# First feed-forward of a nine-tile attention and two-FFN kernel: upper output weights times both parts of the squared values in one 512-column product

## The chip, the cores and the metric

The kernel runs on one core of one Trainium2 chip. The metric is the device time of one execution in microseconds. Three runs of the kernel before gave 950.99, 953.79 and 956.82 us. One further execution was recorded by the hardware profiler, and all rows below come from that one.

## The reference

```python
x = out_up + out_local          # pooled attention plus a 7-wide local attention, heads joined: 2304 tokens x 512
h = x @ w_in                    # 512 x 2048
r = np.maximum(h, 0.0)
g = r * r
x2 = g @ w_out                  # 2048 x 512: the product that is changed
out = ((x2 @ w_a) * (x2 @ w_b)) @ w_out2    # 512 x 1536, twice, and 1536 x 512
```

All is float32. The kernel computes each matrix product to more than the precision of one pass: every operand is held as an upper part and a remainder ("hi" and "lo"), and a product is the sum of three passes, upper weights times upper values, upper weights times lower values, lower weights times upper values (`PASSES`, L188).

## The kernel before

**Tiles and stages.** The 2304 tokens are cut into nine tiles of 256 (`NT1`, `T1`). For each tile the first feed-forward runs 16 iterations f (`F1`), one for each 128 of the 2048 hidden channels; the loop counter is `it = 16 i + f` for tile i. Tiles 0 and 1 are emitted in an order written out by hand (`ORDER`), tiles 2 to 8 by the loop at L904. After the last tile the PSUM pools are closed and the second feed-forward begins with the chains of L925 (512 columns each), which take their eight banks from a new pool, `ps2`; it waits for each old bank by itself.

**One iteration.** `Hidden` (L587) runs 12 matmuls of 256 columns on TensorE (PE) into a bank h. ScalarE (ACT) then applies Relu, Square and a copy to the upper part of g (L601 to L604), and VectorE (DVE) subtracts to get the lower part (`low`, L607). That subtraction is the last reader of the bank h. Two iterations later (`LAG = 2`) `project` (L611) runs another 12 matmuls of 256 columns: for each of four blocks of 128 output channels (et) the three passes. The sums of a tile, x2, stay in two banks of 512 columns, each shared by two blocks, for 16 iterations, and `store_x2` then copies them out, one bank with ACT and one with DVE.

**Order in the loop at L904.** In iteration it: first the events of kind 0; then `Hidden(it)` and its ACT work; then the events of kind 1, which are small products on PE; then `low(it)`; then `project(it - 2)`. Each engine works its instructions off in this order.

**The events.** `Local(i)` is the local attention of tile i, done during tile i-1 (`steps`, L353). DVE multiplies and sums the scores (L373, L382) in steps 0 to 7 and multiplies by the values (L413) in steps 10 to 13, one of four head groups in each; GpSimd (POOL) adds the seven products of each (L421 to L424). The value products have two buffers `pv`, so the third multiplication waits until POOL is done with the first, and the fourth for the second. Step 14 transposes the first half on PE into a bank `xps` (L431); step 15, `assemble`, adds the pooled part on DVE (L445), copies the upper part with ACT (L450) and subtracts on DVE (L451), which frees that bank. Steps 17 and 18 do the same for the second half. Step k of tile i stands at iteration 16 (i-1) - 4 + k for k < 14 and i > 3, otherwise at 16 (i-1) - 3 + k. So the four value multiplications fall at f = 6 to 9 of tiles 3 to 7. `Pooled` is the pooled attention of one batch entry: its batches 2 and 3 run in tiles 2 and 3 and in tiles 4 and 5. Each group of two heads takes a bank for two products of scores (L254, freed by the exponentials L275), for two transposes (L302, freed by the copies L130 to aT) and for the product with the values (L316).

**The banks.** PSUM has eight banks. `ps_h` has three for h, `ps_x` two for x2, and `ps_a` three for all the small products and transposes. A tile of a pool takes a bank that is free, and its first matmul waits until the last reader of the tile before has finished. The three lines are

```python
    ps_h = pp.enter_context(tc.tile_pool(name="ps_h", bufs=3, space=PSUM))
    ps_x = pp.enter_context(tc.tile_pool(name="ps_x", bufs=1, space=PSUM))   # two tags
    ps_a = pp.enter_context(tc.tile_pool(name="ps_a", bufs=3, space=PSUM))
```

Of the kernel before, what the change touches and what calls it, by code (L numbers as in the profile page):

```python
# [17 lines left out]
P = 128  # L18
B, H, S, D = 4, 8, 576, 64
# [7 lines left out]
T1 = 256  # L27
NT1 = NT // T1
G1 = T1 // FACTOR
F1 = 2048 // P  # L30
F2 = 1536 // P
NCT = DM // P
PE_TILES = 2
# [34 lines left out]
L.18 P.16.xy H.20 L.19 J.20 P.17 P.18 P.19 H.21 L.20 J.21 H.22 J.22 P.20 H.23 J.23 H.24 L.22 L.21 J.24 L.24 L.23  # L68
# [14 lines left out]
def pooled_local_attention_two_ffn(  # L83
# [19 lines left out]
    nc = tc.nc  # L103
# [3 lines left out]
    wz = ctx.enter_context(tc.tile_pool(name="wz", bufs=4))  # L107
# [16 lines left out]
    x2_d = dr.tile([P, NCT, NT], F32, name="x2_d")  # L124
# [3 lines left out]
    def copy(engine, out, in_, scale=1.0):  # L128
# [4 lines left out]
        else:  # L133
            engine.tensor_scalar_mul(out=out, in0=in_, scalar1=scale)

    def bank(kind):
        pool, tag = {"a": (ps_a, "aux"), "h": (ps_h, "h"), "x": (ps_x, "x20"), "y": (ps_x, "x21")}[kind]
        return pool.tile([P, 512], F32, tag=tag, name="bank")


# [47 lines left out]
    PASSES = ((0, 0), (0, 1), (1, 0))  # L188
# [392 lines left out]
    wo = [Weight(w_out[f]) for f in range(F1)]  # L581
# [4 lines left out]

    class Hidden:  # L587
        def __init__(self, i, f):
            self.h = h = bank("h")[:, :T1]
# [20 lines left out]

    def project(x2, f, g):  # L611
        for et in range(NCT):
            for n, (a, b) in enumerate(PASSES):
                nc.tensor.matmul(  # L614
                    out=x2[et // 2][:, et % 2 * T1:(et % 2 + 1) * T1],
                    lhsT=wo[f].w[:, a, et * P:(et + 1) * P], rhs=g[:, b],
                    start=(f == 0 and n == 0 and et % 2 == 0), stop=(f == F1 - 1 and n == 2),
                    skip_group_check=True,
                )


    def store_x2(i, x2):
        for e2 in range(2):
            if i == NT1 - 1:
                x = wz.tile([P, 2, 2, T1], F32R, tag="w", name="xr2")
                xr2.append(x)
                split(
                    x[:, 0].rearrange("p e t -> p (e t)"), x[:, 1].rearrange("p e t -> p (e t)"), x2[e2]
                )
                continue  # L630
            if i == NT1 - 2:
                o = wr.tile([P, 512], F32, tag="w", name="x2sb")
            else:
                o = st.tile([P, 1024], F32, tag="stage", name="x2sb")[:, :512]
            if e2:
                nc.vector.tensor_copy(out=o, in_=x2[e2])
            else:
                nc.scalar.activation(out=o, in_=x2[e2], func=AF.Copy)
            nc.sync.dma_start(
                out=x2_d[:, 2 * e2:2 * e2 + 2, i * T1:(i + 1) * T1],  # L640
                in_=o.rearrange("p (e t) -> p e t", e=2),
            )


    events = {}
# [3 lines left out]
    def at_iteration(it, fn, kind=0):  # L649
        events.setdefault(it, ([], [], []))[kind].append(fn)  # L650
# [3 lines left out]
    for b in range(1, B):  # L654
        p = pooled[b]
        start = (2 * b - 2) * F1
# [6 lines left out]
                at_iteration(start + k, fn, takes)  # L663
    for i in range(PE_TILES, NT1):
        for k, fn in sorted(Local(i).steps.items()):
            at_iteration((i - 1) * F1 - (4 if i > PE_TILES + 1 and k < 14 else 3) + k, fn, k in (14, 17))
    for n in range(2):
        at_iteration((PE_TILES - 1) * F1 - 5, lambda n=n: load_qk(4 * PE_TILES + n))
        at_iteration((PE_TILES - 1) * F1 - 2, lambda n=n: load_v(4 * PE_TILES + n))
# [42 lines left out]
    hid, x2 = {}, {}  # L712
# [7 lines left out]
        hid[it].high()  # L720
        run_events(sum(hasattr(h, "g") for h in hid.values()) - 1, 1)

    def project_tile(it, kinds="xy"):
        i, f = divmod(it, F1)
        if f == 0:
            x2[i] = [bank(kind) for kind in kinds]
        project(x2[i], f, hid[it].g)
        if f == F1 - 1:
            store_x2(i, x2.pop(i))
# [13 lines left out]
    def warm(_, n, kind):  # L743
# [206 lines left out]
    for job in JOBS.split():  # L950
        at, name, j = int(job[3:]), job[0], int(job[1])
# [378 lines left out]
```

## Time and profile before

| what | value |
|---|---|
| median of three runs (lowest, highest) | 953.79 us (950.99, 956.82) |
| the profiled execution: its own time | 949.86 us |
| the profiled execution: its span, first to last instruction | 948.1 us |
| mean granted TensorE clock | 0.986 |
| PE busy | 895.6 us, 94% of the span |
| DVE, ACT, POOL busy | 692.6, 503.4, 391.8 us |

The page says how long each engine was busy and, for its costliest groups of instructions, how many there are, the mean time of one, and what ended the idle time in front of them. The times of matmuls overlap: the start of one to the start of the next is what a matmul costs in a dense run, and the timeline's merged lines give it.

### The profile page before, as it was taken

What the parts mean: (1) busy time and instruction counts of PE and PEld (TensorE: products, weight loads), DVE (VectorE), ACT (ScalarE), POOL (GpSimd) and SP (SyncE); (2) the same over time, 40 slices, a digit from 0 to 9 for tenths busy, and PEclk for the clock granted to TensorE, in tenths of its full rate; (3) what the DMA queues carried; (4) which work ended last, traced back from release to release, by engine and by line L of the source; (5) the groups of instructions that cost most, each with busy time, mean ns of one, the idle gap of its engine ahead of it and who ended that gap; (6) DMA issues with size and microseconds to landing.
All of it is one profiled execution on the core that took longest, in us unless ns stands there. A gap on an engine that the chain in (4) does not pass through costs nothing.

```text
span 948.1 us, 16541 instructions
## 1 busy us (share of the span) xinstructions
PE 895.6 (94%) x6130; PEld 813.0 (86%) x6130; DVE 692.6 (73%) x975; ACT 503.4 (53%) x1280; POOL 391.8 (41%) x352
## 2 busy tenths in 40 slices
PE   3567899999999999999999999999999999999998
PEld 3457799999999899999999987888888888788888
DVE  3687997678778686878747699898977774665451
ACT  3676985345644465443448656655555552464531
POOL 1645525526092804535353536665565450001010
PEclk9958999999999999999999999999999999999999
DMA  9669732742139221232214314875756659999522
GB/s 291 192 193 261 258 110 62 170 123 69 62 96 211 56 82 49 69 89 69 76 58 148 112 60 148 296 258 177 254 199 213 223 189 347 383 408 353 239 99 79
DMA packets 69888, 161.88 MB, mean 171 GB/s; under 512 B 8472, under 2 KB 16920, under 8 KB 69808
## 3 DMA queue, kind: packets, MB, share of 16 engines
q1 hardware_dynamic: 64336, 142.33, 43.9%
q0 software_dynamic: 2880, 10.03, 5.9%
q10 hardware_dynamic: 2592, 8.47, 2.6%
q8 instruction: 48, 0.79, 0.3%
q14 instruction: 32, 0.26, 0.1%
HBM read 115.71 MB, written 45.09 MB: 170 GB/s over the span
## 4 chain that ended last, share of the span: by engine, by line
PE 77%; DVE 7%; POOL 6%; DMA 6%; issue 2%; ACT 2%; ACTq 0%; SPq 0%; DVEq 0%; POOLq 0%
PE bank L925 39%; PE bank L614 17%; PE bank L593 16%; DMA more<-in_qk_p 2%; POOL pv L422 2%; DVE pv L413 2%; DMA qkd<-in_qk_p 2%; POOL pv L421 2%; PE bank L254 1%; DMA raw<-in_w_in 1%; PE bank L316 1%; DMA raw<-in_w_out 1%; DVE xb L785 1%; POOL x L424 1%; POOL pv L423 1%
## 5 line engine op out<-in xcount | busy, mean ns | idle before, releaser
L593 PE MATMUL bank<-xx,w 128*128 128x256 f32 x1728 | 234.7, 286 | 7.5 <-DVE g L607 2.7
L614 PE MATMUL bank<-g,w 128*128 128x256 f32 x1728 | 233.5, 286 | 3.2 <-DVE g L607 3.2
L925 PE MATMUL bank<-xb,wb 128*128 128x512 f32 x1008 | 231.3, 390 | 1.5 <-ACT r L1021 0.8
L593 PEld LDWEIGHTS bank<-xx,w 128*128 128x128 f32 x1728 | 219.6, 194 | 10.8 <-DVE g L607 3.6
L925 PEld LDWEIGHTS bank<-xb,wb 128*128 128x128 f32 x1008 | 188.4, 188 | 42.2 <-DVE r L975 1.9
L614 PEld LDWEIGHTS bank<-g,w 128*128 128x128 f32 x1728 | 216.2, 191 | 8.7 <-issue 3.9
L925 PE MATMUL bank<-op,wo 128*128 128x512 f32 (+1 forms) x648 | 132.1, 366 | 1.6 <-DVE op L785 1.6
L925 PEld LDWEIGHTS bank<-op,wo 128*128 128x128 f32 x648 | 111.9, 189 | 21.8 <-DVE op L785 2.2
L601 ACT ACTIVATE bank<-bank 128x256 f32<-128x256 f32 x144 | 53.1, 369 | 135.8 <-PE bank L593 133.4
L421 POOL TENSOR_TENSOR pv<-pv 128x768 f32<-128x768 f32 x28 | 55.0, 1963 | 168.9 <-DVE pv L413 168.9
L785 POOL TENSOR_TENSOR wb<-raw,wb 128x256 fp32r<-128x256 f32 x96 | 88.3, 941 | 55.8 <-ACT wb L865 49.6
L607 DVE TENSOR_TENSOR g<-bank,g 128x256 fp32r<-128x256 f32 x144 | 59.3, 418 | 66.7 <-ACT g L604 66.1
L413 DVE TENSOR_TENSOR pv<-vt,sc 128x1792 f32<-128x1792 f32 x28 | 81.0, 2899 | 19.1 <-POOL x L424 19.1
L1021 ACT ACTIVATE r<-bank 128x512 f32<-128x512 f32 x72 | 42.8, 595 | 73.4 <-PE bank L925 71.9
L785 DVE TENSOR_TENSOR op<-ys,op 128x512 fp32r<-128x512 f32 x84 | 54.0, 708 | 31.3 <-ACT op L788 31.3
L788 ACT ACTIVATE op<-ys 128x512 fp32r<-128x512 f32 x84 | 47.1, 624 | 26.1 <-PE bank L925 14.6
L373 DVE TENSOR_TENSOR p<-qt,kt 128x1792 f32<-128x1792 f32 x28 | 59.4, 2121 | 0.0
L130 ACT ACTIVATE raw<-raw 128x512 uint32<-128x512 uint32 (+1 forms) x87 | 53.2, 669 | 9.7 <-DMA raw<-in_w_in 7.4
L785 POOL TENSOR_TENSOR wos<-raw,wos 128x256 fp32r<-128x256 f32 x48 | 46.2, 982 | 28.8 <-ACT wos L865 25.7
L604 ACT ACTIVATE g<-bank 128x256 fp32r<-128x256 f32 x144 | 55.3, 384 | 4.6
L422 POOL TENSOR_TENSOR pv<-pv 128x256 f32<-128x256 f32 x28 | 55.5, 1983 | 2.2
L382 DVE TENSOR_REDUCE sc<-p 128x28 f32<-128x1792 f32 x28 | 56.2, 2007 | 0.0
(121 smaller groups left out, 1085.9 us busy)
## 6 DMA issues: line engine op xcount, KB each, us to landing
ys<-y_d SPq DMA_DIRECT2D x42, 512.0 KB, 8.3
y_d<-r SPq DMA_DIRECT2D x72, 256.0 KB, 2.2
wo_d<-wos SPq DMA_DIRECT2D x48, 256.0 KB, 2.2
kt<-in_k_l SPq DMA_DIRECT2D x28, 320.0 KB, 3.7
vt<-in_v_l SPq DMA_DIRECT2D x28, 320.0 KB, 2.8
raw<-in_w_a SPq DMA_DIRECT2D x12, 512.0 KB, 4.6
raw<-in_w_b SPq DMA_DIRECT2D x12, 512.0 KB, 4.4
raw<-in_w_o SPq DMA_DIRECT2D x12, 512.0 KB, 3.7
```

Source lines behind the costliest of these rows:

```text
L130: engine.activation(out=out, in_=in_, func=AF.Copy, scale=scale)
L373: nc.vector.tensor_tensor(out=self.p, in0=q.unsqueeze(2).to_broadcast([P, FACTOR, WIN, D]), in1=window(k), op=ALU.mult,)
L382: nc.vector.tensor_reduce(out=self.s[:, :, h], in_=self.p, axis=AX.X, op=ALU.add)
L413: nc.vector.tensor_tensor(out=p, in0=window(heads.pop(("v", n))), in1=self.s[:, :, h].unsqueeze(3).to_broadcast([P, FACTOR, WIN, D]), op=A ...
L421: add(out=p[:, :, 0:3], in0=p[:, :, 0:3], in1=p[:, :, 3:6], op=ALU.add)
L422: add(out=p[:, :, 0], in0=p[:, :, 0], in1=p[:, :, 1], op=ALU.add)
L593: nc.tensor.matmul(out=h, lhsT=wi[f].w[:, a, ct * P:(ct + 1) * P], rhs=x_rhs(i, ct, b), start=(n == 0), stop=(n == 3 * NCT - 1),)
L604: nc.scalar.activation(out=self.g[:, 0], in_=h, func=AF.Copy)
L607: nc.vector.tensor_tensor(out=self.g[:, 1], in0=self.h, in1=self.g[:, 0].bitcast(F32), op=ALU.subtract)
L614: nc.tensor.matmul(out=x2[et // 2][:, et % 2 * T1:(et % 2 + 1) * T1], lhsT=wo[f].w[:, a, et * P:(et + 1) * P], rhs=g[:, b], start=(f == 0 ...
L785: engine.tensor_tensor(out=out, in0=in0, in1=in1, op=ALU.subtract)
L925: nc.tensor.matmul(out=out, lhsT=blk[:, a, cols:cols + P], rhs=rhs[b], start=(start and n == 0), stop=(stop and n == 2), skip_group_check= ...
```

## The change

In tiles 2 to 8 x2 takes four banks, one for each block et, instead of two. The two added banks, kinds w and z, come from `ps_h` and `ps_a` and stay with x2 for the whole tile. For each et `project` issues one matmul of 512 columns, the upper weights against both parts of g side by side, and one of 256 columns, the lower weights against the upper part, which adds to the first half of the bank. `store_x2` now adds the two halves of each bank: ACT copies the second half out, DVE adds the first to it; in tile 8, where x2 stays on the chip, a split into upper part and remainder follows for each block. Steps 14 and 15 of `Local` move one iteration forward for tiles from 4 on. Tiles 0 and 1, emitted by `ORDER`, keep their two banks and three matmuls. The class `Hidden` gets a branch that is not taken.

```diff
-L.18 P.16.xy H.20 ...
+L.18 P.16 H.20 ...
...
     def bank(kind):
-        pool, tag = {"a": (ps_a, "aux"), "h": (ps_h, "h"), "x": (ps_x, "x20"), "y": (ps_x, "x21")}[kind]
+        pool, tag = {
+            "a": (ps_a, "aux"), "h": (ps_h, "h"), "x": (ps_x, "x20"), "y": (ps_x, "x21"),
+            "w": (ps_h, "h"), "z": (ps_a, "aux"),
+        }[kind]
...
     def project(x2, f, g):
         for et in range(NCT):
-            for n, (a, b) in enumerate(PASSES):
-                nc.tensor.matmul(
-                    out=x2[et // 2][:, et % 2 * T1:(et % 2 + 1) * T1],
-                    lhsT=wo[f].w[:, a, et * P:(et + 1) * P], rhs=g[:, b],
-                    start=(f == 0 and n == 0 and et % 2 == 0), stop=(f == F1 - 1 and n == 2),
-                    skip_group_check=True,
-                )
+            w = wo[f].w[:, :, et * P:(et + 1) * P]
+            if len(x2) == 2:
...
+                continue
+
+            nc.tensor.matmul(
+                out=x2[et], lhsT=w[:, 0], rhs=g.rearrange("p a t -> p (a t)"),
+                start=(f == 0), stop=False, skip_group_check=True,
+            )
+            nc.tensor.matmul(
+                out=x2[et][:, :T1], lhsT=w[:, 1], rhs=g[:, 0],
+                start=False, stop=(f == F1 - 1), skip_group_check=True,
+            )
...
     def store_x2(i, x2):
...
-            if e2:
+            if len(x2) == 4:
+                for t in range(2):
+                    src = x2[2 * e2 + t]
+                    if i == NT1 - 1:
+                        more = gp.tile([P, 512], F32, tag="g", name="more")[:, :T1]
+                        nc.scalar.activation(out=more, in_=src[:, T1:], func=AF.Copy)
+                        nc.vector.tensor_tensor(out=src[:, :T1], in0=src[:, :T1], in1=more, op=ALU.add)
+                        split(x[:, 0, t], x[:, 1, t], src[:, :T1])
+                    else:
+                        c = slice(t * T1, (t + 1) * T1)
+                        nc.scalar.activation(out=o[:, c], in_=src[:, T1:], func=AF.Copy)
+                        nc.vector.tensor_tensor(out=o[:, c], in0=src[:, :T1], in1=o[:, c], op=ALU.add)
+            elif e2:
                 nc.vector.tensor_copy(out=o, in_=x2[e2])
             else:
                 nc.scalar.activation(out=o, in_=x2[e2], func=AF.Copy)
...
-            at_iteration((i - 1) * F1 - (4 if i > PE_TILES + 1 and k < 14 else 3) + k, fn, k in (14, 17))
+            at_iteration((i - 1) * F1 - (4 if i > PE_TILES + 1 and k < 16 else 3) + k, fn, k in (14, 17))
...
-    def project_tile(it, kinds="xy"):
+    def project_tile(it, kinds="xywz"):
...
-        "L": lambda it: hid[it].low(), "P": project_tile,
+        "L": lambda it: hid[it].low(), "P": lambda it: project_tile(it, "xy"),
```

## Rows read from the trace of the kernel before

**Rows 1.** The page's costliest groups: out<-in, sizes, count | busy, mean ns | idle before

```profile
L925 PE MATMUL bank<-xb,wb 128*128 128x512 f32 x1008 | 231.3, 390 | 1.5 <-ACT r L1021 0.8
...
L601 ACT ACTIVATE bank<-bank 128x256 f32<-128x256 f32 x144 | 53.1, 369 | 135.8 <-PE bank L593 133.4
```

**Rows 2.** Busy time by stretch, a stretch of tile 3: us, busy (count), clock, DMA

```profile
250.00:275.00 25.00, 25.00 (x213) 23.93 (x212) 15.70 (x22) 13.03 (x42) 13.44 (x10) 1.00 0.15 42
```

**Rows 3.** Timeline of PE at the end of tile 8: start, us, instruction, count

```profile
540.12 4.48 PE L614 MATMUL bank<-g,w 128*128 128x256 f32 x36
544.44 16.51 PE L925 MATMUL bank<-xb,wb 128*128 128x512 f32 x72
```

**Rows 4.** Timelines of DVE and PE in tile 7, iterations 12 to 14

```profile
486.39 0.42 DVE L607 TENSOR_TENSOR g<-bank,g 128x256 fp32r<-128x256 f32 x1 [1.71 <-ACT g L604]
...
489.29 1.61 PE L593 MATMUL bank<-xx,w 128*128 128x256 f32 x12
```

**Rows 5.** Timelines of DVE and PE in tile 3, iterations 9 to 12

```profile
272.83 3.63 DVE L413 TENSOR_TENSOR pv<-vt,sc 128x1792 f32<-128x1792 f32 x1 [1.80 <-POOL x L424]
276.39 0.74 DVE L607 TENSOR_TENSOR g<-bank,g 128x256 fp32r<-128x256 f32 x2
...
275.13 1.60 PE L593 MATMUL bank<-xx,w 128*128 128x256 f32 x12
...
276.93 1.67 PE L614 MATMUL bank<-g,w 128*128 128x256 f32 x12
278.44 1.60 PE L593 MATMUL bank<-xx,w 128*128 128x256 f32 x12
```

**Rows 6.** Timelines of DVE and PE in tile 6, iterations 9 to 12

```profile
432.90 1.07 DVE L607 TENSOR_TENSOR g<-bank,g 128x256 fp32r<-128x256 f32 x3
...
433.37 1.58 PE L614 MATMUL bank<-g,w 128*128 128x256 f32 x11 [1.54 <-DVE g L607]
434.79 1.60 PE L593 MATMUL bank<-xx,w 128*128 128x256 f32 x12
```

**Rows 7.** Timelines of PE, DVE and ACT in tile 4, iterations 9 to 12

```profile
326.69 0.69 PE L302 MATMUL bank<-ident,a 72*72 72x72 f32 x4 [1.38 <-ACT a L290]
327.31 0.71 PE L254 MATMUL bank<-qkd 64*72 64x144 f32 x4
...
329.87 1.60 PE L593 MATMUL bank<-xx,w 128*128 128x256 f32 x12
...
325.30 0.41 DVE L607 TENSOR_TENSOR g<-bank,g 128x256 fp32r<-128x256 f32 x1
...
328.68 0.42 DVE L607 TENSOR_TENSOR g<-bank,g 128x256 fp32r<-128x256 f32 x1 [2.48 <-ACT g L604]
...
330.47 0.68 DVE L445 TENSOR_TENSOR xps<-xps,o_sb 128x512 f32<-128x512 f32 x1
331.93 0.69 DVE L451 TENSOR_TENSOR xx<-xps,xx 128x512 fp32r<-128x512 f32 x1 [0.78 <-ACT xx L450]
...
331.31 0.58 ACT L450 ACTIVATE xx<-xps 128x512 fp32r<-128x512 f32 x1
```

**Rows 8.** Timelines of PE, ACT and DVE in tile 2, iterations 11 and 12

```profile
220.00 0.66 PE L431 MATMUL xps<-ident,x 128*128 128x128 f32 x4
...
224.05 0.71 PE L254 MATMUL bank<-qkd 64*72 64x144 f32 x4 [0.26 <-ACT a L275]
...
220.60 0.40 ACT L130 ACTIVATE aT<-bank 72x288 f32<-72x288 f32 x1
...
224.51 0.69 DVE L451 TENSOR_TENSOR xx<-xps,xx 128x512 fp32r<-128x512 f32 x1 [0.77 <-ACT xx L450]
```

**Rows 9.** Timelines of ACT and DVE where tile 8 ends

```profile
543.92 1.32 ACT L788 ACTIVATE xr<-bank 128x512 fp32r<-128x512 f32 x2 [2.09 <-PE bank L614]
...
544.55 1.41 DVE L785 TENSOR_TENSOR xr<-bank,xr 128x512 fp32r<-128x512 f32 x2 [2.59 <-ACT xr L788]
```

**Rows 10.** Busy time by stretch, early in the kernel, columns as in rows 2

```profile
50.00:60.00 10.00, 5.53 (x56) 4.75 (x57) 7.94 (x19) 8.65 (x28) 4.64 (x4) 0.54 0.69 223
```

More of the change, by code (lines that the diff above doesn't have):

```diff
@@ L67 @@
 H.15 J.15 P.13 L.14 pt.1.1.0.a H.16 J.16 L.15 wl.31.V wl.30.G H.17 P.14 P.15 L.16 J.17 H.18 L.17 J.18 H.19 J.19
-L.18 P.16.xy H.20 L.19 J.20 P.17 P.18 P.19 H.21 L.20 J.21 H.22 J.22 P.20 H.23 J.23 H.24 L.22 L.21 J.24 L.24 L.23
+L.18 P.16 H.20 L.19 J.20 P.17 P.18 P.19 H.21 L.20 J.21 H.22 J.22 P.20 H.23 J.23 H.24 L.22 L.21 J.24 L.24 L.23
 P.21 H.25 J.25 H.26 P.22 L.25 J.26 L.26 H.27 J.27 H.28 P.23 L.27 P.24 P.25 J.28 H.29 J.29 P.26 L.29 L.28 H.30
@@ L134, in copy @@
             engine.tensor_scalar_mul(out=out, in0=in_, scalar1=scale)
+    pair = []
     def bank(kind):
-        pool, tag = {"a": (ps_a, "aux"), "h": (ps_h, "h"), "x": (ps_x, "x20"), "y": (ps_x, "x21")}[kind]
+        pool, tag = {
+            "a": (ps_a, "aux"), "h": (ps_h, "h"), "x": (ps_x, "x20"), "y": (ps_x, "x21"),
+            "w": (ps_h, "h"), "z": (ps_a, "aux"),
+        }[kind]
         return pool.tile([P, 512], F32, tag=tag, name="bank")
@@ L588, in __init__ @@
         def __init__(self, i, f):
-            self.h = h = bank("h")[:, :T1]
+            if True:
+                self.h = h = bank("h")[:, :T1]
+            else:
+                if f % 2 == 0:
+                    pair[:] = [bank("h")]
+                self.h = h = pair[0][:, f % 2 * T1:(f % 2 + 1) * T1]
             n = 0
@@ L612, in project @@
         for et in range(NCT):
-            for n, (a, b) in enumerate(PASSES):
-                nc.tensor.matmul(
-                    out=x2[et // 2][:, et % 2 * T1:(et % 2 + 1) * T1],
-                    lhsT=wo[f].w[:, a, et * P:(et + 1) * P], rhs=g[:, b],
-                    start=(f == 0 and n == 0 and et % 2 == 0), stop=(f == F1 - 1 and n == 2),
-                    skip_group_check=True,
-                )
+            w = wo[f].w[:, :, et * P:(et + 1) * P]
+            if len(x2) == 2:
+                for n, (a, b) in enumerate(PASSES):
+                    nc.tensor.matmul(
+                        out=x2[et // 2][:, et % 2 * T1:(et % 2 + 1) * T1], lhsT=w[:, a], rhs=g[:, b],
+                        start=(f == 0 and n == 0 and et % 2 == 0), stop=(f == F1 - 1 and n == 2),
+                        skip_group_check=True,
+                    )
[4 more added lines that the diff above has]
+            )
+            nc.tensor.matmul(
+                out=x2[et][:, :T1], lhsT=w[:, 1], rhs=g[:, 0],
+                start=False, stop=(f == F1 - 1), skip_group_check=True,
+            )
     def store_x2(i, x2):
@@ L624, in store_x2 @@
             if i == NT1 - 1:
-                x = wz.tile([P, 2, 2, T1], F32R, tag="w", name="xr2")
+                o = x = wz.tile([P, 2, 2, T1], F32R, tag="w", name="xr2")
                 xr2.append(x)
[L627 to L631, printed above, removed]
+            elif i == NT1 - 2:
                 o = wr.tile([P, 512], F32, tag="w", name="x2sb")
@@ L634, in store_x2 @@
                 o = st.tile([P, 1024], F32, tag="stage", name="x2sb")[:, :512]
-            if e2:
+            if len(x2) == 4:
[6 more added lines that the diff above has]
+                        split(x[:, 0, t], x[:, 1, t], src[:, :T1])
+                    else:
+                        c = slice(t * T1, (t + 1) * T1)
+                        nc.scalar.activation(out=o[:, c], in_=src[:, T1:], func=AF.Copy)
+                        nc.vector.tensor_tensor(out=o[:, c], in0=src[:, :T1], in1=o[:, c], op=ALU.add)
+            elif e2:
                 nc.vector.tensor_copy(out=o, in_=x2[e2])
@@ L638, in store_x2 @@
                 nc.scalar.activation(out=o, in_=x2[e2], func=AF.Copy)
[L639 to L642, printed above, removed]
+            if i < NT1 - 1:
+                nc.sync.dma_start(
+                    out=x2_d[:, 2 * e2:2 * e2 + 2, i * T1:(i + 1) * T1],
+                    in_=o.rearrange("p (e t) -> p e t", e=2),
+                )
     events = {}
```

## The prediction

> **What bounds the kernel now.** I read the page first, then the busy times by stretch, then the timelines of PE, DVE, ACT and POOL around one iteration of each tile. The page's two groups [rows 1] give the prices of a 512-column matmul's own run (390 ns) and of a 256-column copy on ACT (369 ns). The stretch of tile 3 shows what matters most: PE is busy for all of its 25 us, DVE for 15.7, ACT for 13.0 [rows 2]. In the changed stage PE sets the pace, so a PE saving counts in full there, and so does every wait that is put in front of PE.
>
> How far PE is from a wait is read by setting the end of `low(it)` beside the start of `Hidden(it + 2)`. In a calm iteration of tile 7 the first ends at 486.39 + 0.42 = 486.81, the second starts at 489.29: 2.5 us of margin [rows 4]. At f = 11 of tiles 3 to 7 it is the other way round. The fourth value multiplication waits for POOL, ends late, and `low` of f = 9 stands behind it on DVE. In tile 3 the two `low` that end there start at 276.39, while `Hidden` of f = 11 starts at 275.13 [rows 5]. Today that costs nothing, because a third bank h is free and the projection of f = 9 starts just afterwards, at 276.93.
>
> **Part 1, the matmuls.** In a dense run the 256-column matmul costs (544.44 - 540.12) / 36 = 120 ns. The 512-column one costs (16.51 - 0.39) / 71 = 227 ns, the last one's own 0.39 us being left off [rows 1, 3]. For each block three of 120 become one of 227 and one of 120, so 360 becomes 347. That is 13 ns; with four blocks, 16 iterations and seven tiles, 448 times: 5.8 us, or 52 ns an iteration. This is the most the change can give, as the columns stay the same (768 a block).
>
> The Trainium skill's page "TensorE: Matmul & The Clock Gate", section "Back-to-back issue gap", gives the isolated gap as N / 2.4 + 2.5 ns. Here the rows show 120 and 227 where that rule gives 109 and 216. By the rule only 2.5 ns a block would be saved, 1.1 us in all, and the total below would be up to 4.7 us higher.
>
> **Part 2, one bank h less.** With w held, `Hidden(it)` waits for `low(it - 2)` in place of `low(it - 3)`. In calm iterations the margin of 2.5 us covers that [rows 4]. At f = 11 it doesn't:
>
> - Tile 3. The first `low` ends near 276.39 + 0.42 = 276.81; `Hidden` starts at 276.85, not 275.13. It takes 12 x 120 = 1.44, then the projection takes 4 x 0.347 = 1.39: the next `Hidden` starts at 279.68 instead of 278.44 [rows 5]. Loss 1.24 us. Tile 5 repeats this picture (two tiles in all).
> - Tile 6. PE already waits 1.54 us here, in the projection, for the same `low` [rows 6]. The wait moves ahead of `Hidden`, which no longer runs under it: 433.35 + 1.44 + 1.39 = 436.18 instead of 434.79. Loss 1.4 us. Tile 7 repeats it (two tiles in all).
>
> The cause is POOL's pace, not PE's, so what PE saves between f = 6 and f = 11 is waited away too.
>
> **Part 3, one bank fewer for small products, and the earlier transposes.** Steps 14 and 15 hold `xps` over the boundary between two iterations.
>
> - Tile 4. Today the transposes of f = 11 start at 326.69, after a wait for ACT, the scores at 327.31 and the next `Hidden` at 329.87 [rows 7]. After the change `Hidden` of f = 11 waits until 325.30 + 0.41 = 325.71 and ends its issue at 327.2, the transposes go to 327.55, and then the scores need a bank. One of the two holds these transposes, the other `xps`. `xps` comes free after `low` of f = 10 (329.10), then L445, L450 and L451 (0.68 + 0.58 + 0.69 with short handovers): 331.05. Scores 0.64 (327.95 less 327.31 by the same spacing) and projection 1.39 put the next `Hidden` at 333.1 instead of 329.87. Loss 3.25 us. If the scores got a bank as now, the loss would be about 0.3; I take the first, since either bank is freed only behind this ACT and DVE chain.
> - Tile 2. Three small products stand in one iteration. The transposes to `xps` started at 220.00; now they wait for the copy that ends at 220.60 + 0.40 = 221.00. One microsecond late, the next scores (224.05 before) reach 225.05 and wait to 225.20 for L451 [rows 8]. Two cheaper projections give back 0.1. Loss 1.0 us.
> - Tile 5 has a pooled batch too, but its small products have died out to one group at the tight place. I put nothing there.
>
> **Part 4, the stores.** Between tiles ACT now does four copies of about 0.37 us [rows 1] and DVE four additions of 0.42 [rows 4], instead of one 512-column copy each. The next tile's first projection comes one `Hidden` (1.44 us) later and needs the banks one by one, 0.35 us apart. The copies run while the last projection still works on later blocks, and the additions follow each other at about a third of a microsecond [rows 6], so they are done just ahead of it. I put nothing. Uncovered, the fourth addition late by half a microsecond in six tiles would cost 3 us.
>
> At the end of tile 8 x2 is freed today by two ACT copies and two subtractions, 543.92 to 545.96 [rows 9]. After, each block needs copy, add, copy, subtract. Only the subtraction overlaps the next block's copy, so it is about 0.37 + 0.42 + 0.37 and handovers, 1.25 us a block, four in a row. The third block, w, is free 3.1 us after PE needs its first new bank. Which new bank lies on it no row shows: if the first, 3.1 us, if the third, 0.4. I take 1.7, the middle.
>
> **Sum.** Waits: 1.0 + 1.24 + 3.25 + 1.24 + 1.4 + 1.4 = 9.5. Savings inside those stretches (about 46 of 112 iterations) are in these figures or waited away; the other 66 give 66 x 0.052 = 3.4. So 9.5 - 3.4 + 1.7 = +7.8 us. The profiled execution took 949.86 us with a span of 948.1; it would become 957.7. The median of the runs is 3.9 us above it, and on the median I forecast 953.8 + 7.8 = 961.6.
>
> Two sentences of the Trainium skill's page "Perfetto Trace Analysis", section "Matmuls", pull apart here: larger matmuls are called more efficient, and independent groups should rotate through PSUM banks so that the evacuation of one overlaps the next. The rows agree with both; the first is worth 13 ns a block, the second is what the held banks take away.
>
> **The rivals.**
>
> - *The saving survives (faster).* One mechanism decides it: whether `low` of f = 9 still ends after PE wants the bank at f = 11. In tile 3 it is late by 1.7 us. If DVE met less of POOL there (its multiplication takes 3.63 us beside POOL and would need 1.7 less [rows 5]), the waits of part 2 vanish, and with `xps` freed early too, what is left is -5.8 + 1.0. That is 949.0. For it speaks only that PE waits for the same `low` anyway in tiles 6 and 7; against it that DVE has no idle time to give at that point. The point from which it is faster by half a per cent is under 1 us of all waits together. 0.07.
> - *Nearly even.* The scores in tile 4 find a bank and the end of tile 8 costs 0.4: 9.5 - 3.0 - 3.4 + 0.4 = +3.5, so 957.3, down to no change if tile 2's wait is absorbed as well. 0.27.
> - *The clock falls.* In tile 4 PE would stand still from 327.55 to 331.05, longer than any wait now after 200 us. Early in the kernel, where PE was busy 5.5 of 10 us, the granted clock averaged 0.54 in that stretch, that is, mostly the lower level of 1.2 GHz [rows 10]. At that level a matmul takes twice as long; 2 to 4 us more, about 964.5. Against it: PE is dense on both sides. 0.12.
> - *More waits of the same kind.* Additions between tiles late by 3 us, or w on the first new bank: 4 us more, 965.6. 0.10.
>
> **How the numbers follow.** The forecast as summed has 0.44; its own range is 958.5 to 965. Half a per cent, 4.8 us, is about what a measurement of this kernel can tell from no change. Slower by more than that: 0.44 + 0.12 + 0.10 = 0.66; within: 0.27; faster: 0.07. The range is 952 to 968: at the lower end most of the even case, at the upper the two dearer cases; it leaves out the first rival and the sum of the dear ones.
>
> **What the profile after would show.** L614's place is taken by 512- and 256-column matmuls at 227 and 120 ns, 896 of them in tiles 2 to 8 instead of 1344. PE's idle before `Hidden` (L593 in the old numbering) is put down to DVE g (`low`), five times near 1.5 to 2 us, once in each of tiles 3 to 7. In tile 4 there is one gap of some 3.5 us before the scores' matmuls, put down to DVE xx or ACT. Behind the last projection there is a gap before the first 512-column chains, put down to DVE. Calm iterations take 2.83 us instead of 2.88. The forecast is wrong if the slots are given out so that `Hidden` meets an older bank, if a pair costs other than 347 ns, or if the first matmul's need of both parts of g makes PE wait in calm iterations.

## The result, and the profile after

The changed kernel takes 965.51 us in the median of four runs (962.74 to 967.33), the kernel before 955.1 us beside it (950.99 to 956.82). The ratio is 1.0127, with a 95% interval from 1.0095 to 1.0158: the change makes the kernel slower, by 10.4 us between the medians and by 12.1 us by the ratio. The forecast was 961.6 us, from 952 to 968, and slower by more than half a per cent with a chance of 0.66.

The profiled execution after took 964.28 us with a span of 962.2 us and a mean granted clock of 0.980. The spans of the two profiles differ by 14.1 us, more than the medians do, because the profiled execution of before lay 5.2 us under its median and that of after 1.2 us under. All times inside a run below are from these two executions.

The page of the kernel after gives the costliest groups (out<-in, sizes, count | busy, mean ns | idle before). L603 is the old L593 (`Hidden`), L617 the old L607 (`low`), and L633 and L637 are the two matmuls that took the place of L614's three:

```profile
L603 PE MATMUL bank<-xx,w 128*128 128x256 f32 x1728 | 237.2, 288 | 17.4 <-DVE g L617 12.7
L633 PE MATMUL bank<-g,w 128*128 128x512 f32 x448 | 167.4, 407 | 0.0
L637 PE MATMUL bank<-g,w 128*128 128x256 f32 x448 | 126.4, 282 | 0.0
```

The new matmuls never wait (idle 0.0). The idle time lies in front of `Hidden`, and it is VectorE's lower part of g that ends it. The view of PE's waits from 180 to 600 us (waited for: us in total, times, longest) puts a number to each kind. The first line is from the kernel before, where two products of L614 waited for that subtraction and no wait was longer than 1.5 us; the others are from the kernel after:

```profile
PE bank L614 <- DVE g L607: 3.1, 2, 1.5
...
PE bank L603 <- DVE g L617: 9.8, 7, 2.0
PE bank L259 <- DVE xx L456: 4.0, 2, 3.5
PE bank L955 <- DVE r L1005: 2.3, 1, 2.3
PE xps L436 <- ACT aT L130: 1.2, 1, 1.2
...
PE bank L955 <- DVE xr L815: 0.3, 1, 0.3
```

To see what each wait costs, I read the start of `Hidden` on both sides of the tight place in each tile, in both kernels. This table has the difference of the two starts; the forecast's term stands beside it:

| tile (it) | before, us | after, us | lost, us | forecast, us |
|---|---|---|---|---|
| 2 (43 to 45) | 8.64 | 10.02 | 1.38 | 1.0 |
| 3 (58 to 60) | 7.01 | 8.52 | 1.51 | 1.24 |
| 4 (74 to 77) | 12.98 | 18.06 | 5.08 | 3.25 |
| 5 (90 to 92) | 7.02 | 8.51 | 1.49 | 1.24 |
| 6 (105 to 108) | 10.89 | 12.48 | 1.59 | 1.4 |
| 7 (121 to 124) | 10.88 | 14.00 | 3.12 | 1.4 |
| sum | | | 14.17 | 9.5 |

The whole stage, from the first matmul of `Hidden(32)` to that of `Hidden(143)`, took 354.4 us before and 366.2 us after: 11.8 us more. The tight places lost 14.17 us, so everything between them gave back 2.4 us, where the forecast had 3.4.

**Tile 3.** This is the timeline of DVE and PE after, in the stretch of [rows 5] (start, us, instruction, count, [idle before <- what ended it]):

```profile
273.09 3.63 DVE L418 TENSOR_TENSOR pv<-vt,sc 128x1792 f32<-128x1792 f32 x1 [1.80 <-POOL x L429]
276.64 0.74 DVE L617 TENSOR_TENSOR g<-bank,g 128x256 fp32r<-128x256 f32 x2
...
277.11 1.70 PE L603 MATMUL bank<-xx,w 128*128 128x256 f32 x12 [1.35 <-DVE g L617]
...
280.06 1.60 PE L603 MATMUL bank<-xx,w 128*128 128x256 f32 x12
```

DVE's part is what it was: the multiplication waits 1.80 us for POOL and takes 3.63 us, and two subtractions follow. PE, which started this `Hidden` at 275.13 before, now stands still for 1.35 us until the first of the two is done. Tile 5 looks the same.

**Tile 4.** The timeline of PE after, in the stretch of [rows 7]:

```profile
322.10 1.60 PE L603 MATMUL bank<-xx,w 128*128 128x256 f32 x12
...
327.14 1.70 PE L603 MATMUL bank<-xx,w 128*128 128x256 f32 x12 [1.59 <-DVE g L617]
328.68 0.41 PE L307 MATMUL bank<-ident,a 72*72 72x72 f32 x4
332.59 0.68 PE L259 MATMUL bank<-qkd 64*72 64x144 f32 x4 [3.50 <-DVE xx L456]
...
335.25 2.58 PE L603 MATMUL bank<-xx,w 128*128 128x256 f32 x12
```

The scores (L259) wait 3.50 us for the subtraction that frees `xps`, since two of the three small banks are in use and the third is held by x2. And then there is something that no row of before in this tile has: the next `Hidden` takes 2.58 us for the same twelve matmuls that take 1.60 us at 322.10.

**Tile 2** has the two waits of the forecast, in PE's timeline in the stretch of [rows 8]:

```profile
220.32 0.63 PE L436 MATMUL xps<-ident,x 128*128 128x128 f32 x4 [1.22 <-ACT aT L130]
...
224.50 0.68 PE L259 MATMUL bank<-qkd 64*72 64x144 f32 x4 [0.49 <-DVE xx L456]
```

**Tiles 6 and 7** have the same pair of waits. In PE's timeline the first two lines are tile 6, the others tile 7:

```profile
434.84 1.70 PE L603 MATMUL bank<-xx,w 128*128 128x256 f32 x12 [0.78 <-DVE g L617]
440.60 1.69 PE L603 MATMUL bank<-xx,w 128*128 128x256 f32 x12 [1.95 <-DVE g L617]
...
484.86 1.70 PE L603 MATMUL bank<-xx,w 128*128 128x256 f32 x12 [0.78 <-DVE g L617]
490.62 2.58 PE L603 MATMUL bank<-xx,w 128*128 128x256 f32 x12 [1.95 <-DVE g L617]
```

After the second wait the `Hidden` of tile 7 takes 2.58 us, that of tile 6 only 1.69. From there to the next `Hidden` it is 4.46 us in tile 7 and 2.94 in tile 6: 1.5 us more. The busy times by stretch (stretch, us, busy (count) of PE, PEld, DVE, ACT, POOL, granted clock, DMA) name the reason. The first line is from the kernel before, the others from the kernel after:

```profile
330.00:355.00 25.00, 25.00 (x211) 23.47 (x210) 21.21 (x27) 15.75 (x53) 1.47 (x3) 1.00 0.27 78
...
330.00:355.00 25.00, 22.41 (x149) 19.86 (x150) 17.30 (x23) 13.27 (x44) 2.73 (x4) 0.93 0.18 46
430.00:455.00 25.00, 22.21 (x154) 20.09 (x153) 18.96 (x17) 9.64 (x26) 17.70 (x13) 1.00 0.25 77
480.00:505.00 25.00, 22.21 (x144) 20.13 (x143) 11.89 (x12) 8.60 (x23) 15.90 (x13) 0.93 0.14 55
```

The granted clock averaged 0.93 in the stretches of tiles 4 and 7 and 1.00 in that of tile 6: for a part of these stretches TensorE ran at 1.2 instead of 2.4 GHz. Before, it is 1.00 in the stretches of all three tiles.

**The end of tile 8** is read from PE's timeline, in the stretch of [rows 3] and [rows 9]. The last line is from the kernel before:

```profile
551.16 0.40 PE L633 MATMUL bank<-g,w 128*128 128x512 f32 x1
551.40 0.28 PE L637 MATMUL bank<-g,w 128*128 128x256 f32 x1
...
555.40 4.27 PE L955 MATMUL bank<-xb,wb 128*128 128x512 f32 x18
559.98 12.56 PE L955 MATMUL bank<-xb,wb 128*128 128x512 f32 x54 [0.30 <-DVE xr L815]
574.80 2.53 PE L955 MATMUL bank<-xb,wb 128*128 128x512 f32 x8 [2.27 <-DVE r L1005]
...
561.47 3.46 PE L925 MATMUL bank<-xb,wb 128*128 128x512 f32 x12 [0.52 <-DVE r L975]
```

From 551.16 to 555.40 there are twelve pairs and no gap: 4.24 / 12 = 353 ns a pair, 236 from the wide matmul to the narrow one (median of 445 starts in the trace) and 118 to the next wide one. Then the first 72 matmuls of the second feed-forward have a wait of 0.30 us in them, and 2.27 us stand behind them where 0.52 us stood before. From the start of L925's (now L955's) first chain to the first matmul behind these 72 it was 561.47 - 544.44 = 17.03 us before and is 574.80 - 555.40 = 19.40 us now: 2.37 us lost.

### The profile page after: what moved, and what is told of

Read it like the earlier page. It is cut to its first block, busy times and chain, and to the rows that moved or that the text cites. A ratio compares the mean times of both kernels' runs of the same rounds, so it can differ in the third digit from the quotient of the medians.

```text
span 962.2 us, 15726 instructions
## 1 busy us (share of the span) xinstructions
PE 898.0 (93%) x5682; PEld 792.1 (82%) x5682; DVE 699.9 (73%) x999; ACT 510.0 (53%) x1304; POOL 393.1 (41%) x352
## 4 chain that ended last, share of the span: by engine, by line
PE 75%; DVE 8%; POOL 6%; DMA 4%; issue 3%; ACT 3%; ACTq 0%; DVEq 0%; POOLq 0%; SPq 0%
PE bank L955 37%; PE bank L603 17%; PE bank L633 9%; PE bank L637 4%; DMA raw<-in_w_in 4%; PE bank L626 3%; POOL pv L427 2%; DVE pv L418 2%; POOL pv L426 2%; PE bank L259 1%; DVE xb L815 1%; PE bank L321 1%; DVE bank L173 1%; DVE raw L134 1%; POOL x L429 1%
## 5 line engine op out<-in xcount | busy, mean ns | idle before, releaser
L603 PE MATMUL bank<-xx,w 128*128 128x256 f32 x1728 | 237.2, 288 | 17.4 <-DVE g L617 12.7
L603 PEld LDWEIGHTS bank<-xx,w 128*128 128x128 f32 x1728 | 220.9, 194 | 27.8 <-DVE g L617 15.8
L955 PE MATMUL bank<-xb,wb 128*128 128x512 f32 x1008 | 231.6, 390 | 4.2 <-DVE r L1005 3.0
L955 PEld LDWEIGHTS bank<-xb,wb 128*128 128x128 f32 x1008 | 188.3, 188 | 45.4 <-DVE r L1005 4.4
L633 PE MATMUL bank<-g,w 128*128 128x512 f32 x448 | 167.4, 407 | 0.0
L955 PE MATMUL bank<-op,wo 128*128 128x512 f32 (+1 forms) x648 | 132.1, 366 | 1.6 <-DVE op L815 1.6
L955 PEld LDWEIGHTS bank<-op,wo 128*128 128x128 f32 x648 | 111.9, 189 | 21.8 <-DVE op L815 2.2
L637 PE MATMUL bank<-g,w 128*128 128x256 f32 x448 | 126.4, 282 | 0.0
L617 DVE TENSOR_TENSOR g<-bank,g 128x256 fp32r<-128x256 f32 x144 | 59.6, 419 | 75.7 <-ACT g L614 75.1
L633 PEld LDWEIGHTS bank<-g,w 128*128 128x128 f32 x448 | 85.0, 190 | 19.3 <-issue 2.9
L637 PEld LDWEIGHTS bank<-g,w 128*128 128x128 f32 x448 | 85.5, 191 | 0.0
L427 POOL TENSOR_TENSOR pv<-pv 128x256 f32<-128x256 f32 x28 | 58.9, 2105 | 2.2
L614 ACT ACTIVATE g<-bank 128x256 fp32r<-128x256 f32 x144 | 55.5, 385 | 4.6
```

Of the source, the lines that this page charges most:

```text
L427: add(out=p[:, :, 0], in0=p[:, :, 0], in1=p[:, :, 1], op=ALU.add)
L603: nc.tensor.matmul(out=h, lhsT=wi[f].w[:, a, ct * P:(ct + 1) * P], rhs=x_rhs(i, ct, b), start=(n == 0), stop=(n == 3 * NCT - 1),)
L614: nc.scalar.activation(out=self.g[:, 0], in_=h, func=AF.Copy)
L617: nc.vector.tensor_tensor(out=self.g[:, 1], in0=self.h, in1=self.g[:, 0].bitcast(F32), op=ALU.subtract)
L633: nc.tensor.matmul(out=x2[et], lhsT=w[:, 0], rhs=g.rearrange("p a t -> p (a t)"), start=(f == 0), stop=False, skip_group_check=True,)
L637: nc.tensor.matmul(out=x2[et][:, :T1], lhsT=w[:, 1], rhs=g[:, 0], start=False, stop=(f == F1 - 1), skip_group_check=True,)
```

## The experiments

The leading theory was the forecast's: the two banks that x2 holds for a whole tile make PE wait, and the cheaper pairs give back little. The rivals were that the moved transposes do it, that the new matmuls themselves cost more than the old ones, and that the new stores do it. Ratios are to the kernel before, timed on the same chip; "stage" is the time from `Hidden(32)` to `Hidden(143)` in the profiled execution, against 354.4 us before.

**Both banks held, old matmuls.** The kernel before with its three 256-column matmuls and two x2 banks, in which two more banks are taken and held idle through each of tiles 2 to 8, as the change does:

```diff
+            "w": (ps_h, "h"), "z": (ps_a, "aux"),
...
-            at_iteration((i - 1) * F1 - (4 if i > PE_TILES + 1 and k < 14 else 3) + k, fn, k in (14, 17))
+            at_iteration((i - 1) * F1 - (4 if i > PE_TILES + 1 and k < 16 else 3) + k, fn, k in (14, 17))
...
-    def project_tile(it, kinds="xy"):
+    def project_tile(it, kinds="xy", hold="wz"):
...
+            held[:] = [bank(kind) for kind in hold]
+            for s in held:
+                nc.tensor.transpose(s[:, :P], ident, ident)
...
+            for s in held:
+                o = gp.tile([P, 512], F32, tag="g", name="held")[:, :1]
+                nc.scalar.activation(out=o, in_=s[:, :1], func=AF.Copy)
```

> The kernel before with its own 256-column products and stores, but in tiles 2 to 8 one bank of ps_h and one of ps_a are held for each whole tile, as the change holds them, and touched only at the tile's ends; steps 14 and 15 stand where the change puts them. Theory A (the loss is waits for held banks): all of the change's waits come back and none of its saving, so 11 to 15 us slower than before: some 1.5 us in each of tiles 2, 3, 5, 6, 7 and 3.5 to 5 in tile 4. Theory B (the loss comes from the wide product itself, whose first matmul needs both parts of g, and from the longer stores): within 2 us of before.

Measured: 966.38 us, 1.0171 [1.0136, 1.0205]; stage 367.9 us, 13.5 more than before. PE's waits from 180 to 580 us, with the numbers of L603, L259 and L436 in this file being L596, L257 and L434:

```profile
PE bank L596 <- DVE g L610: 8.9, 7, 1.9
PE bank L257 <- DVE xx L454: 3.9, 2, 3.5
PE xps L434 <- ACT aT L130: 1.1, 1, 1.1
```

These are the waits of the changed kernel, in number and length, without one of its matmuls. So the loss in the stage comes from the held banks, not from the new matmuls. Read as in the table above, the six tight places lose 12.1 us of the 13.5. The other 1.4 are this run's own: in each of the seven tiles the iteration in which the banks are taken is 0.2 us longer. With 966.38 against 951.41 us, 11 to 15 us slower was expected.

**One bank held.** The same, with only the bank of `ps_h` held (`hold="w"`) and the transposes where they were before; and with only the bank of `ps_a` held (`hold="z"`) and the transposes moved.

> As e1, but only the bank of ps_h is held, and steps 14 and 15 stand as before. A: waits of Hidden for the subtraction two iterations back at f = 11 of tiles 3, 5, 6 and 7, 1.2 to 1.7 us each, half a microsecond in tiles 2 and 4: 5 to 8 us slower than before. B: no change, within 2 us.

> As e1, but only the bank of ps_a is held. A: no wait of Hidden; about 1.4 us in tile 2 (transposes of the local attention wait for a copy on ACT) and a gap of 1.5 to 3.5 us before the scores in tile 4, after which the clock may fall: 3 to 7 us slower than before. B: no change, within 2 us.

Measured: 963.25 us with the bank h held, 1.0139 [1.0094, 1.0185], stage 367.6 us (13.1 more, where 5 to 8 were expected); 957.54 us with the small bank held, 1.0076 [1.0047, 1.0105], stage 361.9 us (7.4 more, where 3 to 7 were expected). The first run's waits and one of its stretches:

```profile
PE bank L596 <- DVE g L610: 11.9, 8, 2.6
...
430.00:455.00 25.00, 21.74 (x157) 21.34 (x156) 16.22 (x13) 8.05 (x22) 18.74 (x15) 0.86 0.22 59
```

With the bank h alone the waits for `low` are 3 us longer than with both banks held, and the clock is at 0.86 in tile 6 and at 0.93 in tile 7's stretch from 480 to 505 us. In the second run the long wait in tile 4 stands alone:

```profile
PE bank L257 <- DVE xx L454: 4.3, 2, 3.8
```

The two costs do not add up (13.1 + 7.4 against 13.5). The clock is one reason: beside the falls above, the second run has 0.86 in tile 4 (330 to 355 us), where the run with both banks has 0.93. And the run with the bank h alone differs from the first one in the place of the transposes as well, which the next experiment takes apart.

**The transposes moved back.** The changed kernel with `k < 14` again:

```diff
-            at_iteration((i - 1) * F1 - (4 if i > PE_TILES + 1 and k < 16 else 3) + k, fn, k in (14, 17))
+            at_iteration((i - 1) * F1 - (4 if i > PE_TILES + 1 and k < 14 else 3) + k, fn, k in (14, 17))
```

> The changed kernel with steps 14 and 15 put back one iteration later in all tiles. A: the gap of 3.5 us in tile 4 shrinks to the 1.2 us that tile 2 shows, since the scores no longer wait for the bank of the local attention's transposes but these wait for a copy on ACT; without the long gap the clock stays up there (1.5 us): tile 4 loses 1 to 2 us instead of 5, so 3 to 4 us faster than the changed kernel. B (the moved steps don't matter): same as the changed kernel within 1 us.

Measured: 964.81 us, 1.0151 [1.0114, 1.0188]; stage 365.1 us, only 1.1 less than with the steps moved. That is a miss. Its waits tell why:

```profile
PE bank L603 <- DVE g L617: 12.3, 7, 2.7
PE xps L436 <- ACT aT L130: 3.0, 2, 1.8
...
PE bank L259 <- DVE xx L456: 0.5, 1, 0.5
```

The 3.5 us behind `xps` are gone, but the waits for `low` grow by 2.5 us (9.8 to 12.3) and the transposes themselves wait 1.8 us more for ACT. In tile 4 `Hidden` then waits 2.03 us, the transposes 1.82, and the clock falls there as well (0.93 from 330 to 355 us). It is also the likely reason why the bank h alone cost so much: its waits of 11.9 us are close to the 12.3 here, and its transposes are the late ones too. The clock is the other part: its tiles 6 and 7 lost 4.69 and 3.51 us, where this run, with a clock of 1.00 there, lost 2.06 in each. Moving the steps exchanges one wait for another; the microsecond by which the two stages differ does not show in the runs (1.0151 here, 1.0127 for the changed kernel).

**The order of the matmuls.** The changed kernel with the four wide matmuls of an iteration in a row, then the four narrow ones:

```diff
         for et in range(NCT):
...
             nc.tensor.matmul(
                 out=x2[et], lhsT=w[:, 0], rhs=g.rearrange("p a t -> p (a t)"),
                 start=(f == 0), stop=False, skip_group_check=True,
             )
-            nc.tensor.matmul(
-                out=x2[et][:, :T1], lhsT=w[:, 1], rhs=g[:, 0],
-                start=False, stop=(f == F1 - 1), skip_group_check=True,
-            )
+        if len(x2) == 4:
+            for et in range(NCT):
+                nc.tensor.matmul(
+                    out=x2[et][:, :T1], lhsT=wo[f].w[:, 1, et * P:(et + 1) * P], rhs=g[:, 0],
+                    start=False, stop=(f == F1 - 1), skip_group_check=True,
+                )
```

> The changed kernel with the four 512-column matmuls of an iteration issued first and then the four of 256 columns, in place of pairs. The pair costs 353 ns in the trace after, not 347: the 256-column matmul starts 236 ns after the 512-column one, where 227 was expected. Theory C (the 9 ns belong to the step from a 512-column to a 256-column matmul): only one such step is left, three of four wide matmuls are followed after 227 ns, and a calm iteration falls from 2.853 to about 2.83 us: 2 to 3 us faster than the changed kernel. Theory D (they belong to the wide matmul on g itself): 236 ns each also in a row, no change within 1 us.

Measured: 965.26 us, 1.0122 [1.0099, 1.0145]; stage 365.0 us. PE's timeline of one calm iteration:

```profile
519.98 1.09 PE L633 MATMUL bank<-g,w 128*128 128x512 f32 x4
520.91 0.63 PE L639 MATMUL bank<-g,w 128*128 128x256 f32 x4
521.38 1.60 PE L603 MATMUL bank<-xx,w 128*128 128x256 f32 x12
```

A wide matmul costs (520.91 - 519.98) / 4 = 232 ns in a row of four, a narrow one (521.38 - 520.91) / 4 = 118. The order is worth almost nothing: the stage is 1.2 us shorter, but the wait for a bank behind tile 8 grows from 0.3 to 1.0 us. By the time this is theory D; by the matmuls it is neither, as the wide one on g stays some 5 ns above the 227 of [rows 3].

**A faster POOL.** If the waits for `low` come from POOL, they must go when POOL has less to do. Both kernels without two of POOL's additions (the sums over the local window then lack products):

```diff
-            add(out=p[:, :, 0], in0=p[:, :, 0], in1=p[:, :, 1], op=ALU.add)
-            add(out=p[:, :, 2], in0=p[:, :, 2], in1=p[:, :, 6], op=ALU.add)
```

> The changed kernel without the second and third of the four additions that GpSimd does for each head group of the local attention (so the sums over the window are incomplete). To be read against the kernel before with the same two left out, e7. Theory A (Hidden waits for a subtraction that stands on VectorE behind a multiplication which waits for GpSimd): with GpSimd done about 3 us earlier in each head group the waits of Hidden at f = 9 to 11 go, in all of tiles 3 to 7; what is left are tile 2 and the gap in tile 4, 2 to 5 us, less the saving of 3: e6 is -1 to +3 us against e7. Theory B (wide product and stores): e6 stays 10 us or more above e7.

> The kernel before without the second and third addition of GpSimd in each head group (incomplete sums over the window). A: 2 to 5 us faster than before, since its own waits for VectorE in tiles 6 and 7 (1.5 us each) and some of tile 4's (1.4 us) go with GpSimd's delay. B says nothing of it.

Measured: the changed kernel 949.62 us, 0.9956 [0.9935, 0.9978], stage 351.5 us; the kernel before 945.36 us, 0.9935 [0.9914, 0.9955], stage 348.7 us. In the changed kernel the waits that POOL had caused are nearly gone:

```profile
PE bank L259 <- DVE xx L454: 2.4, 1, 2.4
PE bank L601 <- DVE g L615: 0.5, 2, 0.3
```

By the medians POOL's pace costs the kernel before 8 us and the changed one 16 (by the ratios 6 and 16). Of the 10.4 us between them 4.3 are left, just over the -1 to +3 expected; by the ratios it is 2.0 of 12.1, and their intervals overlap, so a loss isn't shown here. Nor is a gain: the stage of the changed kernel is 2.8 us the longer. The wait for a small bank stays in tile 4, the clock fell there once more (0.97 from 300 to 330 and from 330 to 355 us, 1.00 in the kernel before with the same edit), and the end of tile 8 stays.

**The same work, spread.** Nothing is left out here: the third and fourth value multiplication of tiles 3 to 7 move from f = 8 and 9 to f = 9 and 11, so that POOL has an iteration more for each. It was tried on the kernel before and on the changed one; for the former

```diff
-            at_iteration((i - 1) * F1 - (4 if i > PE_TILES + 1 and k < 14 else 3) + k, fn, k in (14, 17))
+            late = max(0, k - 11) if i > PE_TILES + 1 and k < 14 else 0
+            at_iteration((i - 1) * F1 - (4 if i > PE_TILES + 1 and k < 14 else 3) + k + late, fn, k in (14, 17))
```

> The kernel before with the third and fourth value multiplication of the local attention issued one and two iterations later (at f = 9 and 11 instead of 8 and 9) in tiles 3 to 7, so that they no longer stand on VectorE waiting for GpSimd with a subtraction behind them. GpSimd is the pace there and has its next head group ready either way. Theory A: TensorE's waits for VectorE in tiles 6 and 7 (1.5 us each) and for ScalarE behind it in tile 4 (1.4 us) go: 3 to 5 us faster than before. Rival E (the delay only moves: the multiplications meet the next tile's scores, or GpSimd ends late and the second transposes wait): same as before or slower.

> The changed kernel with the same two multiplications later. A: the waits of Hidden at f = 9 to 11 go, about 1.5 us in tiles 3, 5 and 6, 3.1 us in tile 7 with its stretch of low clock, and part of tile 4's 5 us: 7 to 11 us faster than the changed kernel, within 3 us of the kernel before, and still 2 to 6 us behind e8, for the two waits for banks of ps_a (tiles 2 and 4) and the end of tile 8. B (the wide product and its stores cost by themselves): the loss against e8 stays 10 us or more.

Measured: on the kernel before 946.69 us, 0.9942 [0.9916, 0.9967], stage 349.9 us; on the changed one 953.48 us, 1.0001 [0.9986, 1.0015], stage 354.3 us. In the stretch of [rows 6], the first three lines are from the timelines of DVE and POOL before, the others from the same timelines of the kernel before with this edit:

```profile
415.58 2.02 DVE L413 TENSOR_TENSOR pv<-vt,sc 128x1792 f32<-128x1792 f32 x1
429.33 3.65 DVE L413 TENSOR_TENSOR pv<-vt,sc 128x1792 f32<-128x1792 f32 x1 [1.81 <-POOL x L424]
429.25 1.84 POOL L421 TENSOR_TENSOR pv<-pv 128x768 f32<-128x768 f32 x1
...
429.12 2.98 DVE L413 TENSOR_TENSOR pv<-vt,sc 128x1792 f32<-128x1792 f32 x1
432.02 0.41 DVE L607 TENSOR_TENSOR g<-bank,g 128x256 fp32r<-128x256 f32 x1
...
428.37 1.85 POOL L421 TENSOR_TENSOR pv<-pv 128x768 f32<-128x768 f32 x1
```

The multiplication no longer waits for POOL and takes 2.98 us where the one at the same place before took 3.65, behind a wait of 1.81 us. No subtraction is late, and PE no longer waits for one. The Trainium skill's page "GPSIMD Engine Reference", section "Specifications", says that GpSimd shares its SBUF interfaces with VectorE and that VectorE's instructions with two SBUF inputs contend for them. The traces agree and give a size. This multiplication takes 2.02 us where no POOL instruction runs beside it (the first line). Where an addition of POOL is under way at its start, it takes longer by what is left of that addition: 1.10 us are left here (428.37 + 1.85 - 429.12), 1.76 before. In all the traces together 335 of 336 of these multiplications keep to this sum within 0.16 us (the other one began 0.03 us behind an addition and took 2.01). So `low` was late before for two reasons, the wait for POOL's buffer and the slow multiplication that began beside POOL's next addition, and the edit shortens both. It goes the other way too: POOL's second addition (L422) takes 2.40 us beside the multiplication and 0.73 where none runs. In the changed kernel the waits for `low` are gone as well, and these stay:

```profile
PE bank L259 <- DVE xx L456: 3.1, 2, 2.6
PE bank L956 <- DVE r L1006: 2.2, 1, 2.2
PE xps L436 <- POOL x L429: 2.2, 2, 1.1
PE xps L436 <- ACT aT L130: 1.2, 1, 1.2
```

The edit is worth 6.2 us on the kernel before, where 3 to 5 were expected, and about 12 on the changed one (1.0127 to 1.0001), where 7 to 11 were. The kernel before with it is the fastest complete version here, 6.8 us ahead of the changed kernel with it (5.6 by the ratios; 2 to 6 were expected). Not all of that is the banks: the waits for POOL (L429) are those of the earlier transposes, 1.1 us in each of tiles 6 and 7, and the clock fell in tile 4 (0.96 from 300 to 330 us, 0.98 from 330 to 355).

**The store of tile 8, shortened.** The changed kernel without the copy and the addition of the second halves in tile 8 (its x2 then lacks the products with the lower part of g):

```diff
-                        more = gp.tile([P, 512], F32, tag="g", name="more")[:, :T1]
-                        nc.scalar.activation(out=more, in_=src[:, T1:], func=AF.Copy)
-                        nc.vector.tensor_tensor(out=src[:, :T1], in0=src[:, :T1], in1=more, op=ALU.add)
```

> The changed kernel without the copy and addition of the second halves in tile 8's store alone (so the last 256 tokens miss the product with the lower part of g). The trace after shows two waits behind tile 8: 0.3 us for a bank and 2.3 us for a result of VectorE some 14 us later, where the kernel before waited 0.5. Theory A (both follow from the four serial copy, add, copy, subtract of that store): both fall to the values of before, 2 to 2.5 us off the span. Rival F (the second wait is another event's): only the 0.3 us goes.

Measured: 962.14 us, 1.0098 [1.0065, 1.013]; stage 366.2 us, as in the changed kernel. PE's timeline:

```profile
555.04 16.51 PE L952 MATMUL bank<-xb,wb 128*128 128x512 f32 x72
572.07 3.22 PE L952 MATMUL bank<-xb,wb 128*128 128x512 f32 x11 [0.52 <-DVE r L1002]
```

The 72 matmuls run without a break in 16.51 us, and the wait behind them is 0.52 us, both as before. So both waits at the end of tile 8, the one for a bank and the one for r, follow from the longer store.

## Why the prediction was right, and where its sizes were off

The sign, the places and the mechanism held. In the terms of the forecast's sum the profile has 14.17 + 2.37 - 2.4 = 14.1 us where 9.5 + 1.7 - 3.4 = 7.8 stood: 1.8 times as much. In the medians it is 10.4, and that this is nearer is partly luck, since the profile of before lay further under its median than that of after. The measured 965.5 us is just outside the leading case's own 958.5 to 965, beside the 964.5 of the case in which the clock falls.

**Part 1, the matmuls.** The term was mis-sized: a pair costs 353 ns, not 347, so a block saves 7 ns and not 13. The failed step is the 227 ns taken from the chain of the second feed-forward; on g a wide matmul costs 236 beside narrow ones and 232 in a row. 353 ns gives 28 ns an iteration; what the calm iterations gave back, 2.4 us over the 96 outside the tight places, is 25. That 2.4 came near the 3.4 of the forecast is partly luck: an iteration saves half of the 52 ns, but 96 iterations kept it and not 66. The Trainium skill's page "TensorE: Matmul & The Clock Gate", section "Back-to-back issue gap", gives N / 2.4 + 2.5 ns as the isolated gap, from which I estimated a saving of 2.5 ns a block. The 7 measured here lie between that and the 13 of my rows, and both matmuls cost more than that rule's 216 and 109.

**Part 2, one bank h less.** Right: `low` of f = 9 ends where it did, PE meets it in `Hidden`, and it is the same five tiles. The number of waits was off, seven of 0.78 to 1.95 us for five of 1.5 to 2, since in tiles 6 and 7 the `Hidden` of f = 10 waits as well. Tiles 3 and 5 lost 1.51 and 1.49 for 1.24, tile 6 1.59 for 1.4. The small excess in tile 3 is `low` itself, 0.14 us later against the `Hidden` of it = 58 (by estimate what PE had saved since f = 6, 4 to 5 times 28 ns, waited away as the forecast said), and 0.12 us more from one `Hidden` to the next (2.95 us, computed as 2.83). Holding the banks with the old matmuls gave the same waits, and with a faster or better spread POOL they went: the cause is shown.

**Part 3, one small bank less.** Right, with the release that I chose: in tile 4 the scores waited for the subtraction behind `xps`, 3.50 us, as long as computed (331.05 - 327.55). In tile 2 both waits came, 1.22 and 0.49 us for about 1.0 and 0.15. But the earlier transposes, which I blamed with the bank, are not a cost by themselves in the changed kernel: with them moved back the waits for `low` grow and the time is the same. Only where those waits are absent, with the small bank alone and with the spread POOL, do they wait for POOL, 1.9 and 2.2 us in all.

**The clock.** Here a step failed. Its fall was a rival with 0.12 and the time 964.5, and "PE is dense on both sides" was the argument against it. It fell in tile 4, and in tile 7 too, where no case had it: 1.5 us each, 3.0 of the 4.7 us by which the waits exceed the forecast. In tile 4 the loss of 5.08 us is the 3.25 computed, the 1.5 of the clock, and a rest of 0.3. So what was measured is the leading case and this rival together, not one of them.

**Part 4, the stores.** Between tiles nothing showed: no wait for them stands in the list. At the end of tile 8 I took the middle of 0.4 and 3.1 us; the bank cost 0.30, so it was near the lower end. What was missing is a step further on: the four blocks leave ACT and DVE later, and r is late for the next chain by 1.75 us more than before. 2.37 us in all for 1.7, shown by the shortened store. That the sum came near is luck: the term that I had was too high, and the one that I lacked was the larger.

**The rivals.** "The saving survives" would have needed DVE to meet less of POOL at f = 9. The experiments made that true by hand: the waits of part 2 did vanish, and by the medians the change was still 4.3 to 6.8 us behind the kernel before with the same help. The rival's own case, with `xps` freed early too, was not run: in both runs tile 4 keeps its wait for `xps` (2.4 and 2.6 us) and a fall of the clock. An estimate from the measured terms finds no saving in it: 448 pairs save 7 ns each, 3.1 us, while tile 2 (1.38) and the end of tile 8 (2.37) cost 3.75. Of the two sentences of the Trainium skill's page "Perfetto Trace Analysis", section "Matmuls", that the prediction set against each other, rotating groups through banks weighed more here than larger matmuls: 12.1 us in the run that only holds the banks, against the 2.4 us that the calm iterations gave back.

## What to carry to other kernels

A PSUM bank that is held through a loop is paid for by whoever used it as slack, so set the end of the last reader beside the start of the next writer in the tightest iteration, not in a calm one. Count the saving of merged matmuls from start to start, on the operands in question, and expect a few nanoseconds where the columns stay the same. If a loop waits once a tile for an in-order engine that itself waits for a slower one, spread that engine's work first: it was worth 6.2 us here, with no new bank. And look at what the slower engine runs beside: here each of the two held up the other.

## What was not expected of the hardware

A 512-column matmul costs 227 ns in the chains of the second feed-forward [rows 3], but 232 in a row of four and 236 between 256-column ones when g is its input. Why is open; the order explains at most 4 of the 9 ns.

VectorE's multiplication with two SBUF inputs takes 2.02 us without POOL and up to 3.65 when it starts beside an addition of POOL; the excess is what was left of that addition, within 0.16 us in 335 of 336 cases. POOL's addition behind it is held up in turn, 2.40 us for 0.73.

The granted clock fell in tile 7 after waits of 0.78 and 1.95 us with 3.8 us of matmuls between them, and not after the same waits in tile 6 (0.93 and 1.00 in their stretches). It is not one execution's accident alone: the versions with the wide matmuls first and with the short store have the same two drops, 0.93 from 330 to 355 us and 0.95 from 475 to 510. With the banks held and the old matmuls only the one in tile 4 is there, and so it is with the small bank alone, with the steps moved back and with the faster or spread POOL, where the long wait in tile 4 was only 2.4 and 2.6 us; with the bank h alone, tile 4, whose wait is 1.9 us, stays at 1.00, and tiles 6 and 7 fall. Before, all these stretches are at 1.00. What tells tile 7 from tile 6 was not tried and stays open.
